# A retention layer and a Mish MLP on one core: the second tile's k turned back ahead of its outputs, with markers and one transpose moved

## The chip, the core and the metric

The kernel runs on one core of a Trainium2 chip. The metric is the device time of one execution in microseconds (us); lower is better. Engines: PE (TensorE, matmuls; PEld is its weight load), DVE (VectorE), ACT (ScalarE), POOL (GpSimd) and SP (SyncE). POOL and SP issue most of the DMAs. Each engine takes its instructions in the order in which the program gives them, and waits on semaphores for the others.

## The reference

```python
scores = (q @ k.T) / sqrt(64)                 # 8 batches, 8 heads, 576 positions, head size 64
rel = pos[:, None] - pos[None, :]
ret = scores * where(rel >= 0, gamma[h] ** rel, 0)      # gamma[h] = 1 - 2 ** (-5 - h)
x = (ret @ v).transpose(0, 2, 1, 3).reshape(4608, 512)
h = x @ w_in                                  # 512 -> 2048
g = h * tanh(softplus(h))                     # Mish
out = g @ w_out                               # 2048 -> 512, float32
```

## The kernel before

**Work and tiles.** The 4608 rows are 36 chunks of 128, four to a tile, nine tiles (t = 0 to 8). Chunks 0 to 7 are the first 128 positions of each batch; they make tiles 0 and 1 and are computed directly (scores, mask, outputs). The later chunks use a running state per batch: scores inside halves of 64 positions, plus the state times q. Each tile then goes through `g1` (x times w_in by 16 blocks of 128 columns, Mish on ACT) and a second product with w_out: tile 0 by `g2_first`, the others by `unit`, seven products of halves (Strassen) whose sums DVE makes (`g_sum`, L645 to 653, and `w_sum`).

**First chunks.** For tile t, `f_transpose` makes q and k by head, `f_scores` the masked scores, `f_v` (L221) casts v of one chunk from float32 to bf16 (L226), and `f_out` (L229; products at L242) makes the outputs, on L251 copied to the tile's xT. `f_k0` (L259, 16 transposes on PE at L264) turns k back into rows, `f_k0_copy` (L267) copies that from PSUM into two tiles, `first_states` (L277, L289) multiplies it with v, and `first_states_copy` (L297) puts the result into SBUF as the first state. `f_out` for tile 1 and `f_k0` both draw from the two buffers named `sc`. Their letters in the list of steps (L853): T `f_transpose`, S `f_scores`, C `f_mix`, V `f_v`, O `f_out`, F `f_state`. Step i of that list stands ahead of part i of tile 0's `g2_first` (four row blocks s of four parts); `store` copies a finished row block out (L619) and sends it.

**Loads.** `load(n)` (L308) issues chunk n's q, k and v from POOL (L325). From chunk 10 on, a tiny POOL copy stands ahead of it (L313) that waits until the v of chunk n - 2 has landed. The loads of chunks 8 to 11 are given at L843, before tile 0's `g1` and `g2_first`.

**Later chunks.** For chunk n: P (`step_p`, DVE, L341) scales q and k, V (`step_v`, L348) scales v, T (`step_t`, L351) transposes, below chunk 16 on PE (L362) and from 16 on by a DMA that SP issues (L370). A visit (`visit`, or `visit_first` and `visit_second`) makes two chunks' outputs: products L484, then L500 for one set of row halves, a marker, other products, and L500 for the other set; the output copies are L512 on ACT. The marker (`written`, L411) is an empty instruction on SP's queue that waits for the last products of the first set; the first product of the second set waits for the marker (`behind`, L406). `first_states` uses a marker in the same way.

**Order.** It is written out by hand: the loops at L854 (g2 of tile 0), L886 (steps u of tile 1's g1, then tile 1's first units) and L951 (tiles 2 on) give every engine its queue. SP's queue has the transposing DMAs (L370), the sends of output rows (L611) and the markers; POOL's has the loads, the L313 copies, later the V steps and the pacing copies (L949).

Of the kernel before, what the change touches and what calls it, by code (L numbers as in the profile page):

```python
# [10 lines left out]
BF16 = mybir.dt.bfloat16  # L11
# [5 lines left out]
def kernel(  # L17
# [18 lines left out]
    nc = tc.nc  # L36
    B, H, S, D = q.shape
    assert (B, H, S, D) == (8, 8, 576, 64)
    P = 128
    NP = H // 2  # L40
# [5 lines left out]
    NPE = 16  # L46
# [17 lines left out]
    first = ctx.enter_context(tc.tile_pool(name="first", bufs=1))  # L64
    io = ctx.enter_context(tc.tile_pool(name="io", bufs=PF))
    tok = ctx.enter_context(tc.tile_pool(name="tok", bufs=6))
    tr = ctx.enter_context(tc.tile_pool(name="tr", bufs=4))
# [99 lines left out]
    k0 = {}  # L167
# [3 lines left out]
    def f_mix(g, i):  # L171

        name = ("qb", "kb")[i]
        fst[1][name, "mix", g] = room[3][:, ts(i, 1024)].rearrange("p (r x d) -> p r x d", r=8, x=2)
        nc.vector.tensor_copy(fst[1][name, "mix", g].rearrange("p r x d -> p x r d"),
                              fst[1][name][:, ds(2 * g, 2), :].rearrange("p x (r d) -> p x r d", r=8))
# [44 lines left out]
    def f_v(t, b, copy):  # L221
        vb = room[2][:, ts(b, 512)].rearrange("p (h d) -> p h d", h=H)
        copies = copy if isinstance(copy, tuple) else (copy,)
        n = H // len(copies)
        for j, copy in enumerate(copies):
            copy(vb[:, ds(n * j, n), :], v0[4 * t + b][:, ds(n * j, n), :])  # L226
        fst[t]["vb"][b] = vb
# [25 lines left out]
    def f_state(t, b, engine=nc.gpsimd):  # L253

        n = 4 * t + b
        v0s[n] = room[(6, 3)[t]][:, ts(b, H * D)].rearrange("p (h d) -> p h d", h=H)
        engine.tensor_tensor(v0s[n], v0[n], gv[:, 0, :].unsqueeze(2).to_broadcast([P, H, D]), op=OP.mult)

    def f_k0(t):  # L259

        tp = ps_sc.tile([P, 2, H, P], BF16, name="sc")
        for g in range(2):
            for h in range(H):
                nc.tensor.transpose(tp[:, g, h, :], fst[t]["kb", g][:, h, :], ident)  # L264
        return tp

    def f_k0_copy(t, tp, copies):  # L267
        for g in range(2):
            pair = first.tile([P, 2, H, D], BF16, name="k0", bufs=2)
            copies[g](pair.rearrange("p x h d -> p h x d"), tp[:, g].rearrange("p h (x d) -> p h x d", x=2))  # L270
            for x in range(2):
                k0[4 * t + 2 * g + x] = pair[:, x]

    s0 = {}
    s0_banks = {}

    def first_states(t, j):  # L277

        if j == 0:
            s0_banks[t] = [pool.tile([P, 2, NP, 64], F32, name=name)  # L280
                           for pool, name in ((ps_st, "st"), (ps_o, "ops"))]
        made = []
        for x in range(2):
            for p in range(NP):
                for i in range(2):
                    r, b = ds(64 * (i ^ j), 64), 4 * t + 2 * i + x
                    for e in range(2):
                        hh = 4 * (p // 2) + 2 * e + p % 2
                        made.append(nc.tensor.matmul(  # L289
                            s0_banks[t][i][ds(64 * e, 64), x, p, :], lhsT=k0[b][r, hh, :], rhs=v0s[b][r, hh, :],  # L290
                            start=(j == 0 and x == 0 and p == 0), stop=True, skip_group_check=True))
        if j == 0:
            s0_banks[t].append(written(made[-8:]))
        else:
            behind(made[0], s0_banks[t][2])

    def first_states_copy(t, copy):  # L297
        for i in range(2):
            pair = first.tile([P, 2, NP, 64], F32, name="s0", bufs=4)
            copy(pair, s0_banks[t][i])  # L300
            for x in range(2):
                s0[4 * t + 2 * i + x] = pair[:, x]
# [103 lines left out]
    def behind(ins, others):  # L406

        sync = mybir.DependencyInfo(mybir.DependencyClass.Sync, mybir.DependencyReason.DATA)
        tc.add_manual_dep(ins.ins, others.ins.name, sync, reason="row halves and a bank")

    def written(products):  # L411
        sync = mybir.DependencyInfo(mybir.DependencyClass.Sync, mybir.DependencyReason.DATA)
        seen = nc.sync.nop()
        for ins in products:
            tc.add_manual_dep(seen.ins, ins.ins.name, sync, reason="row halves and a bank")
        return seen
# [53 lines left out]
    def run(jobs, *how):  # L470
        while jobs:
            jobs.pop()(*how)
# [152 lines left out]
    NS = 2  # L625
# [39 lines left out]
    dve, act, pool = nc.vector.tensor_copy, nc.scalar.copy, nc.gpsimd.tensor_copy  # L665
# [122 lines left out]
    def att(n, steps):  # L788
        if n >= n_chunks:
            return  # L790
        for step in steps:
            {"P": step_p, "V": step_v, "T": step_t}[step](n)
# [46 lines left out]
    for j in range(2):  # L839
        half = mask[ds(64 * j, 64)]  # L840
# [9 lines left out]
        g1(0, f)  # L850
    for i in range(2):
        f_mix(0, i)
    steps = {0: "T0", 3: "S0 C1", 9: "T1", 11: "S1", 12: "V0 V1 V2 V3", 14: "O0 O1 O2 O3", 15: "F0 F1"}  # L853
    for i in range(nF):  # L854
        for step in steps.get(i, "").split():
            n = int(step[1])
            if step[0] == "T":
                for j in range(2):
                    f_transpose(1, n, j, [(ps_sc, "sc", (dve, act)[j])])
            elif step[0] == "S":  # L860
                f_scores(1, n)
            elif step[0] == "V":
                f_v(1, n, dve if n == 3 else act)
            elif step[0] == "C":
                for j in range(2):
                    f_mix(n, j)
            elif step[0] == "F":
                f_state(1, n, nc.vector)
            else:
                f_out(1, n, (dve, act)[n // 2])  # L870
        g2_first(i // 4, i % 4)
# [10 lines left out]
    ps = {0: 0, 4: 1, 8: 2, 11: 3}  # L882
    vs = {0: 0, 5: 1, 9: 2, 13: 3, 18: 4, 19: 5}
    ts_ = {4: 0, 7: 1, 12: 2, 14: 3, 19: 4, 21: 5}
    FIRST = {1: (0, 0), 2: (1, 0), 3: ("turn", 1), 5: (0, 1), 6: (1, 1)}
    for u in range(24):  # L886
        j, w = divmod(u, 4)
        halved[0] = 2 if u < 1 else 0
        if u in FIRST:
            what, of = FIRST[u]  # L890
            if what == "turn":
                f_k0_copy(of, f_k0(of), (dve, act))
            else:
                first_states(of, what)
                if what:
                    first_states_copy(of, act)
        if u in ps:
            att(N0 + ps[u], "P")
        if u == 11:
            step_m(N0)  # L900
        if u in vs:
            att(N0 + vs[u], "V")
        if u in (1, 2):
            f_state(1, u + 1, nc.vector)
        for what in {7: "W4", 9: "W6 W3 W1", 19: "S1", 21: "S6"}.get(u, "").split():
            w_sum(int(what[1])) if what[0] == "W" else g_sum(1, int(what[1]))
        if w == 0 and j > 0:
            if j < 5:
                load(N0 + j + 3)
            else:  # L910
                more_loads(N0 + j + PF)
        if u == 10:
            units = states(N0)
            units[0]()
            step_s(N0)
            units[1]()
            run(sums)
        elif u == 16:
            att(N0 + 4, "P")
            visit(N0, ((ps_o, "ops"), (ps_h, "hp")), (act, act), masked=False)  # L920
            g_sum(1, 2)
            run(sums)
            att(N0 + 5, "P")
            step_m(N0 + 2)
        elif u == 22:
            visit(N0 + 2, ((ps_h, "hp"), (ps_h, "hp")), (act, act))
        if u in (13, 20):
            run(casts, dve if u == 13 else act)
        if u in ts_:
            att(N0 + ts_[u], "T")  # L930
        if u < nF:
            g1(1, u)
            flush()
        else:
            unit(1, u - nF)


    PLAN, ALONE = ([x.split() for x in y.split("|")] for y in (
        "S2 g0 g1 U0|S1 U1|g2 g3 U2|U3|g4 g5 U4|U5|g6 U6|S6 g7|U7 g8 g9|S5 U8|U9 g10|g11|S7 g12 g13 U10|U11|g14 U12|g15 U13",
        "S2 g0 g1 U0|S1 U1|g2 g3 U2|U3|g4 g5 U4|U5|g6|S6 g7 U6|U7 g8 g9|S5 U8|U9 g10|g11|S7 g12 g13 U10|U11|g14 U12|U13 g15"))  # L940
# [10 lines left out]
    for t in range(NS, nT):  # L951
        for i in range(nF):
            n, w = NCH * (t + 1) + i // 8 * 2, i % 8
# [2 lines left out]
                run(casts, act)  # L956
            if (t, i) in HALVED:
                halved[0] = HALVED[t, i]
            for job in PLAN[i] if t > NS else {5: ("S5",), 8: ("W7",), 9: ("S7",)}.get(i, ()):
                if job[0] == "S":  # L960
                    g_sum(t - 1, int(job[1]))
                elif job[0] == "W":
                    w_sum(int(job[1]))
# [30 lines left out]
            if n + 2 >= NPE and w == (6 if n + 2 == NPE else 3) and n + 4 < n_chunks:  # L994
                tick(t, i)
                att(n + 4, "V")
                att(n + 5, "V")
            if w == 7 and n + 4 == NPE:
                att(n + 5, "T")
            if w == (4 if n <= NPE - 2 else 7) and n + 4 >= NPE:  # L1000
                att(n + 4, "T")
# [65 lines left out]
```

## Time and profile before

| | |
|---|---|
| median of three runs | 290.27 us (290.06 to 297.87) |
| the profiled execution | 289.96 us, span 288.2 us |
| PE busy | 280.8 us, 97% of the span |
| DVE, ACT, POOL busy | 200.1, 156.8, 156.3 us |
| mean granted PE clock | 1.000 |
| PE waits listed | 1.3 us at the start; 0.7, 0.6 and three of 0.2 later |

The span runs from the first to the last instruction; the time of an execution is a little longer. Times in the views count from the span's start. A timeline row has start, duration, engine, source line, operation, output and inputs, and a count of merged instructions; in brackets, the idle time before it and what ended it.

### The profile page before, as it was taken

How to read it: one execution, taken by the hardware profiler on the slowest of the kernel's cores; microseconds unless marked ns; L12 is line 12 of the kernel's file. 1: busy time of each engine (PE TensorE's matmuls, PEld its weight loads, DVE VectorE, ACT ScalarE, POOL GpSimd, SP SyncE). 2: the span in 40 equal slices, each digit the busy share in tenths (PEclk: the TensorE clock that was granted, in tenths of full speed). 3: DMA queues.
4: the chain of work that ended last, by engine and by line, in shares of the span. 5: the costliest groups of instructions: out<-in, count | busy, mean ns of one | idle time of the engine just before them, and what ended most of it. 6: DMA issues, size and time to landing. Idle time of an engine off the chain costs nothing.

```text
span 288.2 us, 8782 instructions
## 1 busy us (share of the span) xinstructions
PE 280.8 (97%) x3812; PEld 188.7 (65%) x3812; DVE 200.1 (69%) x281; ACT 156.8 (54%) x272; POOL 156.3 (54%) x226
## 2 busy tenths in 40 slices
PE   8899999999999999999999999999999999999994
PEld 3466775556876657666766666667666766665783
DVE  4741457999999987895599767975895272533383
ACT  5566414788776564565465555564466446444320
POOL 8686860887793999697929685969140000000000
PEclk9999999999999999999999999999999999999999
DMA  7999999988899994999898994696937001201133
GB/s 150 198 204 205 205 238 220 292 200 197 191 210 196 166 283 121 161 217 196 210 168 184 178 238 136 182 198 182 176 90 131 2 3 73 75 1 73 28 102 93
DMA packets 41543, 45.93 MB, mean 159 GB/s; under 512 B 23840, under 2 KB 31264, under 8 KB 41504
## 3 DMA queue, kind: packets, MB, share of 16 engines
q0 software_dynamic: 14256, 30.15, 49.6%
q1 hardware_dynamic: 26656, 14.69, 26.3%
q8 instruction: 30, 0.49, 0.8%
q10 hardware_dynamic: 592, 0.52, 0.6%
q14 instruction: 9, 0.07, 0.1%
HBM read 36.70 MB, written 9.44 MB: 160 GB/s over the span
## 4 chain that ended last, share of the span: by engine, by line
PE 82%; DMA 12%; POOL 3%; issue 1%; DVE 1%; ACT 0%; POOLq 0%; ACTq 0%
PE hp L570 38%; PE ops L661 30%; DMA room<-in_v_dram 5%; DMA w_out_t<-in_moe_w_out_dram 4%; DMA gT<-in_v_dram 3%; PE hp L661 2%; PE sc L428 2%; POOL gT L107 2%; PE sc L382 2%; PE sc L752 1%; PE st L661 1%; PE hp L575 1%; PE hp L500 1%; PE sc L362 1%; PE hp L484 1%
## 5 line engine op out<-in xcount | busy, mean ns | idle before, releaser
L570 PE MATMUL hp<-xT,w_in_t 128*128 128x512 bf16 x530 | 128.7, 380 | 0.1
L586 ACT ACTIVATE gT<-hp 128x512 bf16<-128x512 f32 x144 | 85.9, 600 | 54.6 <-PE hp L570 53.1
L570 PEld LDWEIGHTS <-w_in_t 128*128 128x128 bf16 x530 | 50.8, 98 | 45.7 <-issue 0.5
L661 PEld LDWEIGHTS <-room 128*128 128x128 bf16 x608 | 58.8, 98 | 14.7
L341 DVE TENSOR_TENSOR qks<-qkraw,gqk 128x512 bf16<-128x512 f32 x56 | 48.1, 909 | 8.9 <-issue 7.4
L652 DVE TENSOR_TENSOR room<-gT 128x2048 bf16<-128x2048 bf16 x40 | 49.5, 1259 | 0.8 <-ACT gT L586 0.8
L661 PE MATMUL ops<-room,room 128*128 128x256 bf16 x336 | 41.7, 273 | 0.0
L949 POOL COPY held<-gT 128x1 bf16<-128x1 bf16 x58 | 24.4, 421 | 31.2 <-ACT gT L586 31.2
L661 PEld LDWEIGHTS <-gT 128*128 128x128 bf16 x256 | 24.5, 98 | 6.2 <-issue 0.2
L388 DVE TENSOR_TENSOR sm<-sc,mask 128x1024 bf16<-128x1024 f32 x14 | 17.1, 1218 | 14.9 <-PE sc L382 12.6
L661 PE MATMUL ops<-w_out_t,room 128*128 128x256 bf16 x224 | 27.1, 273 | 0.0
L348 POOL TENSOR_TENSOR vs<-vraw,gv 128x512 bf16<-128x512 f32 x20 | 26.0, 1320 | 0.0
L325 POOL DMA_DIRECT2D vraw<-in_v_dram x24 | 21.3, 887 | 3.6 <-DMA w_out_t<-in_moe_w_out_dram 2.6
L325 POOL DMA_DIRECT2D qkraw<-in_q_dram x24 | 21.7, 904 | 1.0 <-issue 0.6
L325 POOL DMA_DIRECT2D qkraw<-in_k_dram x24 | 21.2, 883 | 0.0
L452 DVE TENSOR_TENSOR total<-sc,total 128x256 f32<-128x256 f32 x32 | 13.5, 423 | 2.2 <-PE sc L428 1.4
L512 ACT CAST xT<-hp 128x512 bf16<-128x512 f32 x19 | 10.3, 589 | 7.3 <-PE hp L500 7.3
L575 PE MATMUL hp<-xT,w_in_t 128*128 128x256 bf16 x92 | 13.8, 273 | 0.0
L661 PE MATMUL ops<-room,gT 128*128 128x256 bf16 x112 | 13.4, 273 | 0.0
L575 PEld LDWEIGHTS <-w_in_t 128*128 128x128 bf16 x92 | 9.0, 98 | 5.5
L661 PE MATMUL ops<-w_out_t,gT 128*128 128x256 bf16 x96 | 12.3, 273 | 0.0
L696 DVE TENSOR_TENSOR res<-ops,res 128x512 f32<-128x512 f32 x6 | 4.2, 692 | 9.0 <-PE ops L661 9.0
(162 smaller groups left out, 339.8 us busy)
## 6 DMA issues: line engine op xcount, KB each, us to landing
out_dram<-res SPq DMA_DIRECT2D x29, 256.0 KB, 4.7
qkraw<-in_q_dram POOLq DMA_DIRECT2D x24, 256.0 KB, 5.9
qkraw<-in_k_dram POOLq DMA_DIRECT2D x24, 256.0 KB, 6.8
vraw<-in_v_dram POOLq DMA_DIRECT2D x24, 256.0 KB, 6.1
w_out_t<-in_moe_w_out_dram POOLq DMA_DIRECT2D x4, 512.0 KB, 10.2
w_in_t<-in_moe_w_in_dram POOLq DMA_DIRECT2D x3, 512.0 KB, 9.3
out_dram<-res SPq DMA_DIRECT2D x9, 128.0 KB, 2.3
gT<-in_k_dram POOLq DMA_DIRECT2D x8, 128.0 KB, 9.1
```

The costliest lines, as they stand in the source:

```text
L325: nc.gpsimd.dma_start(out=t, in_=src[b, :, ds(P * c, P), :].rearrange("h p d -> p h d"))
L341: nc.vector.tensor_tensor(slots[:, :, y], heads[:, :, y], factors[:, :, y].unsqueeze(3).to_broadcast([P, NP, 2, D]), op=OP.mult)
L348: engine.tensor_tensor(vs, live[n]["v"], gv[:, c, :].unsqueeze(2).to_broadcast([P, H, D]), op=OP.mult)
L388: nc.vector.tensor_tensor(sm.rearrange("p e x n i -> p (e x n) i"), live[n]["sc"].rearrange("p e x n i -> p (e x n) i"), mask.unsqueeze(1) ...
L452: nc.vector.tensor_tensor(new[:, k], st[:, j, x], total[b], op=OP.add)
L512: copy(xts[t][:, :, ds(P * s, 2 * P)].rearrange("p h (x j i) -> p j h x i", x=2, j=2)[:, j], both[j])
L570: nc.tensor.matmul(to, lhsT=w, rhs=x, start=first, stop=last)
L575: nc.tensor.matmul(to[:, ts(j, n)], lhsT=w, rhs=x[:, ts(j, n)], start=False, stop=False, skip_group_check=True)
L586: nc.scalar.activation(gts[t][:, f, :], hp, AX.Mish)
L652: engine.tensor_tensor(to, g_half(t, *a), g_half(t, *b), op=op_)
L661: nc.tensor.matmul(bank[:, half, :], lhsT=g[:, f, ts(half, P)], rhs=w[:, f, :], start=(f == 0 and half == 0 and not add), stop=(f == hF - ...
L949: nc.gpsimd.tensor_copy(held[:, i % 2:i % 2 + 1], gts[t][:, f, 0:1])
```

## The change

1. Tile 1's k is turned back (`f_k0` and `f_k0_copy`) at step 13 of tile 0's g2, between V1 and V2, and not at step u = 3 of tile 1's g1. Both copies are on DVE (before: one DVE, one ACT), into two buffers of the pool `qkT` (before: into the two `k0` buffers that tile 0 uses).
2. V2 and V3 move from step 12 to step 13; V3's cast is on POOL (before: DVE).
3. The markers of the visits stand on ACT's queue; those of `first_states` stay on SP's.
4. In tile 2's loop, chunk 17's T comes at step 5 (before: 7), and the sum S5 at step 6 (before: 5).

```diff
--- before.py
+++ after.py
@@ -266,7 +266,11 @@
 
     def f_k0_copy(t, tp, copies):
         for g in range(2):
-            pair = first.tile([P, 2, H, D], BF16, name="k0", bufs=2)
+            if t == 0:
+                pair = first.tile([P, 2, H, D], BF16, name="k0", bufs=2)
+            else:
+                pair = tr.tile([P, 2, NP, P], BF16, name="qkT", bufs=6)
+                pair = pair.rearrange("p i n t -> p (i n t)").rearrange("p (x h d) -> p x h d", x=2, h=H)
             copies[g](pair.rearrange("p x h d -> p h x d"), tp[:, g].rearrange("p h (x d) -> p h x d", x=2))
             for x in range(2):
                 k0[4 * t + 2 * g + x] = pair[:, x]
@@ -290,7 +294,7 @@
                             s0_banks[t][i][ds(64 * e, 64), x, p, :], lhsT=k0[b][r, hh, :], rhs=v0s[b][r, hh, :],
                             start=(j == 0 and x == 0 and p == 0), stop=True, skip_group_check=True))
         if j == 0:
-            s0_banks[t].append(written(made[-8:]))
+            s0_banks[t].append(written(made[-8:], nc.sync))
         else:
             behind(made[0], s0_banks[t][2])
 
@@ -408,9 +412,9 @@
         sync = mybir.DependencyInfo(mybir.DependencyClass.Sync, mybir.DependencyReason.DATA)
         tc.add_manual_dep(ins.ins, others.ins.name, sync, reason="row halves and a bank")
 
-    def written(products):
+    def written(products, engine=nc.scalar):
         sync = mybir.DependencyInfo(mybir.DependencyClass.Sync, mybir.DependencyReason.DATA)
-        seen = nc.sync.nop()
+        seen = engine.nop()
         for ins in products:
             tc.add_manual_dep(seen.ins, ins.ins.name, sync, reason="row halves and a bank")
         return seen
@@ -850,7 +854,7 @@
         g1(0, f)
     for i in range(2):
         f_mix(0, i)
-    steps = {0: "T0", 3: "S0 C1", 9: "T1", 11: "S1", 12: "V0 V1 V2 V3", 14: "O0 O1 O2 O3", 15: "F0 F1"}
+    steps = {0: "T0", 3: "S0 C1", 9: "T1", 11: "S1", 12: "V0 V1", 13: "K1 V2 V3", 14: "O0 O1 O2 O3", 15: "F0 F1"}
     for i in range(nF):
         for step in steps.get(i, "").split():
             n = int(step[1])
@@ -860,7 +864,9 @@
             elif step[0] == "S":
                 f_scores(1, n)
             elif step[0] == "V":
-                f_v(1, n, dve if n == 3 else act)
+                f_v(1, n, pool if n == 3 else act)
+            elif step[0] == "K":
+                f_k0_copy(n, f_k0(n), (dve, dve))
             elif step[0] == "C":
                 for j in range(2):
                     f_mix(n, j)
@@ -882,18 +888,15 @@
     ps = {0: 0, 4: 1, 8: 2, 11: 3}
     vs = {0: 0, 5: 1, 9: 2, 13: 3, 18: 4, 19: 5}
     ts_ = {4: 0, 7: 1, 12: 2, 14: 3, 19: 4, 21: 5}
-    FIRST = {1: (0, 0), 2: (1, 0), 3: ("turn", 1), 5: (0, 1), 6: (1, 1)}
+    FIRST = {1: (0, 0), 2: (1, 0), 5: (0, 1), 6: (1, 1)}
     for u in range(24):
         j, w = divmod(u, 4)
         halved[0] = 2 if u < 1 else 0
         if u in FIRST:
-            what, of = FIRST[u]
-            if what == "turn":
-                f_k0_copy(of, f_k0(of), (dve, act))
-            else:
-                first_states(of, what)
-                if what:
-                    first_states_copy(of, act)
+            half, of = FIRST[u]
+            first_states(of, half)
+            if half:
+                first_states_copy(of, act)
         if u in ps:
             att(N0 + ps[u], "P")
         if u == 11:
@@ -956,7 +959,7 @@
                 run(casts, act)
             if (t, i) in HALVED:
                 halved[0] = HALVED[t, i]
-            for job in PLAN[i] if t > NS else {5: ("S5",), 8: ("W7",), 9: ("S7",)}.get(i, ()):
+            for job in PLAN[i] if t > NS else {6: ("S5",), 8: ("W7",), 9: ("S7",)}.get(i, ()):
                 if job[0] == "S":
                     g_sum(t - 1, int(job[1]))
                 elif job[0] == "W":
@@ -995,7 +998,7 @@
                 tick(t, i)
                 att(n + 4, "V")
                 att(n + 5, "V")
-            if w == 7 and n + 4 == NPE:
+            if w == 5 and n + 4 == NPE:
                 att(n + 5, "T")
             if w == (4 if n <= NPE - 2 else 7) and n + 4 >= NPE:
                 att(n + 4, "T")
```

## What was predicted

> **What bounds the kernel now.** I read the page first (busy shares, the 40 slices), then who waits for whom with TensorE as the waiter, then the timelines of PE, POOL and DVE around the edited steps. The page first:
>
> ```profile
> span 288.2 us, 8782 instructions
> ...
> PE 280.8 (97%) x3812; PEld 188.7 (65%) x3812; DVE 200.1 (69%) x281; ACT 156.8 (54%) x272; POOL 156.3 (54%) x226
> ...
> PEclk9999999999999999999999999999999999999999
> ```
>
> PE is busy almost everywhere, at full granted clock. Whatever makes PE wait in mid-kernel is added to the end, since nothing later has room to give it back; and there is little idle time to win. In the stage that is edited there is one PE wait. The waits view lists it as 0.6 us on ACT L226, the cast of a first-chunk v (step V2), and the PE timeline shows where it lies:
>
> ```profile
> 44.61 1.89 PE L570 MATMUL hp<-w_out_t,gT 128*128 128x512 bf16 x8
> 46.43 0.64 PE L242 MATMUL sc<-room,room 128*64 128x128 bf16 x16
> 47.70 0.64 PE L242 MATMUL sc<-room,room 128*64 128x128 bf16 x16 [0.63 <-ACT room L226]
> 48.27 1.04 PE L570 MATMUL ops<-w_out_t,gT 128*128 128x512 bf16 x4
> ...
> 53.57 1.06 PE L264 MATMUL sc<-ident,qkT 128*128 128x128 bf16 x16
> ```
>
> L242 at 46.43 is O0 and O1, at 47.70 O2 and O3 (8 matmuls each, so O3 starts near 47.91), L264 at 53.57 is the turned-back k. Eight 128x512 products issue in 44.61 to 46.34, 0.216 us each. Now the engine to which the change hands one cast, POOL:
>
> ```profile
> 42.42 0.88 POOL L325 DMA_DIRECT2D vraw<-in_v_dram  x1 [2.62 <-DMA w_out_t<-in_moe_w_out_dram]
> 50.65 0.63 POOL L313 COPY landed<-vraw 128x1 f32<-128x1 f32 x1 [7.35 <-DMA vraw<-in_v_dram]
> 51.23 0.89 POOL L325 DMA_DIRECT2D qkraw<-in_q_dram  x1
> 52.11 0.88 POOL L325 DMA_DIRECT2D qkraw<-in_k_dram  x1
> 52.98 0.88 POOL L325 DMA_DIRECT2D vraw<-in_v_dram  x1
> 53.86 0.43 POOL L313 COPY landed<-vraw 128x1 f32<-128x1 f32 x1
> 54.23 0.88 POOL L325 DMA_DIRECT2D qkraw<-in_q_dram  x1
> 55.10 0.88 POOL L325 DMA_DIRECT2D qkraw<-in_k_dram  x1
> 55.98 0.88 POOL L325 DMA_DIRECT2D vraw<-in_v_dram  x1
> ```
>
> POOL looks idle from 43.3 to 50.65, but it is not free: it stands at the L313 copy of load(10), waiting for chunk 8's v to land, and everything later in its queue stands behind it. The loads of chunks 8 to 11 (L843) are issued in the program before the g2 loop at L854, so the moved cast V3 comes behind all nine of these rows: the instruction order of the changed kernel has it after the vraw issue of chunk 11. The casts and DVE:
>
> ```profile
> L226 POOL CAST room<-gT x2: 520/566/612, 13.3 to 15.3; 128x512 bf16<-128x512 f32 x1, 128x256 bf16<-128x256 f32 x1
> ...
> L226 DVE CAST room<-room x1: 427/427/427, 47.1 to 47.1; 128x512 bf16<-128x512 f32 x1
> ```
> ```profile
> 43.84 2.35 DVE L219 TENSOR_TENSOR room<-sc,dmask 128x1024 bf16<-128x1024 f32 x2 [1.44 <-PE sc L212]
> 47.07 0.43 DVE L226 CAST room<-room 128x512 bf16<-128x512 f32 x1 [0.88 <-DMA room<-in_v_dram]
> ```
>
> Before, V3 (the DVE row at 47.07) is done at 47.50, ahead of O3.
>
> **The change part by part.**
>
> *V3 on POOL.* The source landed at 46.95, so only POOL's queue counts. POOL is past the last of the nine rows at 55.98 + 0.88 = 56.86. The 128x512 cast takes 0.61 there (the longer of the two L226 POOL casts), so V3 is done at 57.47, and O3 starts 0.05 later (ACT's cast ended at 47.65 and O2 began at 47.70): 57.52 against 47.91. **Delay of PE at O3: 9.6 us.** Behind O3 on PE stand the last two row blocks of g2, all of the next g1 and everything else; DVE and ACT then wait for PE. The chain does not depend on PE: its DMAs and nine POOL rows need nothing made after 46 us. Its bounds: chunk 8's v could land earlier or later (third rival); the second landing, chunk 9's v, has its last piece at 52.84 in the trace's record of landings, 1.0 us before POOL asks for it. Behind V3 on POOL stands the L313 copy for chunk 10, which before ran at 59.07 after 2.2 us of waiting, so it loses nothing.
>
> *The clock after the gap.* PE would stand from about 48.2 (O2's end, below) to 57.5, 9.3 us. The trace's clock record has two entries, 1.0 from 6.34 us on and 0.5 from 289.65, 5.4 us after the last matmul ended. A 9.3 us gap is longer, so I take it that the clock falls and PE restarts at half pace. The price is in the first row of PE:
>
> ```profile
> 1.26 5.26 PE L164 MATMUL ops<-room 128*128 128x512 bf16 x12 [1.26 <-DVE room L126]
> ```
>
> These 12 products took from 1.26 to about 6.35, 5.1 us; at 0.216 each they would have taken 2.6. **Cost 2.5 us**, bounds 0 (the clock stays) and 2.5. I take 2.5, the only cold stretch in the trace. [...]
>
> *The 16 turn-backs (L264), moved from 53.57 to before the second row block of g2's last quarter.* Their 0.89 us (53.57 to 54.46) leaves the path after O3. In the new place, 45.47 to 46.36, they only shorten the wait for V3: **gain 0.9 us**. They need the score buffer that the first L219 frees near 45.0; free. If V3 were on time they would cost what they gain.
>
> *Their two copies.* Both now on DVE, ahead of L251 (before: one on DVE, 0.68, one on ACT, 1.01, off the path). O2 and O3 take the same score buffer as the turn-backs, so O2 now waits for the copies: DVE ends L219 at 46.19, copies out a row block (L619, 0.68), then two of 0.68, done near 48.0. O1 ends near 47.74, so O2 waits some 0.3 us. Cover: the wait for V3; 0 on the path, 0.3 if that cover is gone. V2's old wait is gone too (ready 47.65), which the 9.6 already holds.
>
> *The copies' new buffers.* Two more of the six qkT buffers are drawn; what they held was last read by the first tile's scores, before 20 us. Later transposes draw buffers whose readers are done. Cost 0, the range of it nothing.
>
> *Markers on ACT.* Fourteen markers of the visits go from SP's queue to ACT's; the two of the first states stay. On SP they made PE wait once, some 0.08 us at 98.93. On ACT a marker stands behind whatever ACT has not finished: before the second half at 77.71 ACT's last copy ends at 77.69, at 156.13 at 156.15; elsewhere it is 0.1 us or more ahead. What is queued behind the marker on ACT, the visit's own output copies (L512), needs later matmuls anyway. Bounds -0.1 to +0.6 (one ACT copy in the way once); I take +0.1. SP's transposes and sends, freed of these waits, wait for DVE as before.
>
> *Chunk 17 sooner, S5 after it.* The transposing DMA on SP now follows P17 at step 5 instead of 7; its readers come near 99 and it landed before that already: 0. But S5 (L652) now stands behind P17 on DVE:
>
> ```profile
> 86.53 1.22 DVE L652 TENSOR_TENSOR room<-gT 128x2048 bf16<-128x2048 bf16 x1
> 87.67 1.29 DVE L341 TENSOR_TENSOR qks<-qkraw,gqk 128x512 bf16<-128x512 f32 x2
> ```
>
> Swapped, S5 ends near 86.5 + 1.2 + 1.2 = 88.9, and the products that read it began at 88.79: +0.1 (0 to 0.8, the latter if P17's rows landed late).
>
> **Sum.** 9.6 + 2.5 - 0.9 + 0.1 + 0.1 = +11.4 us on the profiled execution's 289.96 us (span 288.2): **301.4 us**. Its time is 0.3 us under the median of the three runs, 290.27; against that it is 3.8% more.
>
> **Rivals.**
> *The clock does not fall.* Same wait, warm restart: 301.4 - 2.5 = 298.9. For it: no mid-kernel gap in this trace shows a fall. Against: the end of the trace does, after 5.4 us. 0.08.
> *A second landing waits too.* If the DMA of chunk 9's v takes what the slowest vraw took (13.5 us from issue to landing, median 6.1), it lands at 56.8, not 52.84; POOL goes on 2.9 us later, and so does O3: 304.3. Against: its landing is on record and nothing ahead of it changes but one earlier store. 0.10.
> *The other side: chunk 8's v lands before POOL asks.* If it were there by 43.3, the rows from 50.65 to 56.86 (6.2 us) and the cast would end at 50.1, O3 would be 2.3 us late, the gap too short for the clock: 289.96 + 2.3 - 0.9 + 0.2 = 291.6, no change. It decides at a landing near 46.7, 4 us earlier than now, where the gap gets under 5.4 us and the total under 2%. Against: the same loads queue ahead of it as before. 0.05.
> *The change does what it looks like.* POOL takes V3 at 46.95 as if its queue were empty: O2 starts near 48.1 for the copies, g2 goes on 0.4 us later than before, and 0.9 is saved: 289.7. Only if the order on POOL were another. 0.01.
>
> **How the numbers follow.** The forecast has 0.76. The range, 298.5 to 304.3, takes in the warm restart below and the late second landing above, and the small terms. 2% (5.8 us) is about what a measurement of this kernel can tell from no change. Slower by over 2%: 0.76 + 0.08 + 0.10 = 0.94. Within 2%: 0.05. Faster: 0.01.
>
> **What would show it.** Right: in the changed profile a PE wait of some 9 us at L242 on POOL L226, that cast on POOL near 57 behind nine unchanged rows, a digit under 9 in PEclk near 58, 128x512 products at 0.43 us for some 5 us, and the rest of PE's timeline shifted by about 11 us without new gaps. The turn-backs stand near 45.5 with both copies on DVE. Wrong: V3 on POOL before 52, or later PE gaps above 0.5 us at L500 (markers) or at the products of S5 near 100.

## The result, and the profile after

The changed kernel takes 300.67 us (median of six runs) against 290.16 us before (six runs): 1.034 times as long, 95% interval 1.030 to 1.038. 301.4 was predicted, with a range from 298.5 to 304.3. The profiled execution took 300.16 us (span 298.5) against 289.96 (288.2). Some executions of most kernels here, the kernel before among them, were disturbed and ran up to 20 us longer; all ratios below leave those out, and so may differ from a ratio of medians.

The changed kernel's page and its list of PE's waits (us in total, times, longest):

```profile
PEclk9999999599999999999999999999999999999998
```
```profile
PE sc L242 <- POOL room L226: 8.2, 1, 8.2
```

PE has one long wait, 8.2 us for POOL's cast; the next in the list are 1.3 us at the start and 0.5. The granted clock is low in the slice from 52 to 60 us (each slice is 7.5 us). Lines of the changed kernel below the edit are four higher than before (L325 is L329, L313 is L317, L570 is L574). PE's timeline comes first, then POOL's. The last view has two stretches, each with its length, the busy times of PE, PEld, DVE, ACT and POOL, then the granted clock (0.50 and 1.00), the DMA share and GB/s:

```profile
45.07 1.06 PE L264 MATMUL sc<-ident,qkT 128*128 128x128 bf16 x16
...
46.92 0.64 PE L242 MATMUL sc<-room,room 128*64 128x128 bf16 x16
47.73 0.41 PE L242 MATMUL sc<-room,room 128*64 128x128 bf16 x8 [0.17 <-ACT res L623]
56.38 0.64 PE L242 MATMUL sc<-room,room 128*64 128x128 bf16 x8 [8.24 <-POOL room L226]
```
```profile
49.86 0.19 POOL L317 COPY landed<-vraw 128x1 f32<-128x1 f32 x1 [8.33 <-DMA vraw<-in_v_dram]
...
52.95 0.20 POOL L317 COPY landed<-vraw 128x1 f32<-128x1 f32 x1
...
55.70 0.63 POOL L226 CAST room<-room 128x512 bf16<-128x512 f32 x1
```
```profile
56.38:61.00 4.62, 4.29 (x18) 1.91 (x20) 2.13 (x4) 1.43 (x2) 3.10 (x5) 0.50 0.97 208
61.00:66.00 5.00, 4.95 (x91) 2.74 (x91) 5.00 (x9) 3.53 (x8) 3.73 (x4) 1.00 0.88 271
```

The order is the one foreseen: turn-backs, O0 and O1, O2, then eight microseconds of nothing, because V3 on POOL has its turn only after two landing waits and six issues. Behind the wait PE runs at half clock for 4.6 us. The trace's clock record has it low from 50.78, 2.6 us after O2's end, to 61.02.

Where the time went is best seen from three marks on PE: O3's first product, the first product of L500 in the first visit, and the last product of all. The columns are the time of O3, then the two stretches, in us (differences of start times in the profiled executions; "gap filled" and the others are the experiments below):

| kernel | O3 | O3 to first visit | first visit to last product |
|---|---|---|---|
| before | 47.95 | 21.72 | 214.34 |
| changed | 56.38 | 23.07 | 214.81 |
| changed, second profile | 56.56 | 23.43 | 214.69 |
| only V3 on POOL | 56.21 | 24.16 | 214.94 |
| two loads behind V3 | 48.10 | 20.86 | 214.85 |
| one load behind V3 | 53.78 | 23.49 | 217.48 |
| gap filled, second profile | 56.83 | 20.85 | 217.38 |
| turn-backs, V3 on ACT | 47.89 | 20.95 | 215.15 |

Changed less before: 8.43 + 1.35 + 0.47 = 10.25 us, the whole difference of the spans (10.2). (The second profile is of the same kernel in another run, below.) In the second column stand two terms: without the turn-backs at their old place and at full clock it is 20.9 (three kernels), so they give back 0.8 to 0.9 and the half clock costs 2.2 to 2.6. That fits the clock record: 4.6 us of work at a clock of 0.50 would lose 2.3.

### The profile page after: what moved, and what is told of

It reads as the page before. It is cut to its first block, busy times and chain, and to the rows that moved or that the text cites. A ratio compares the mean times of both kernels' runs of the same rounds, so it can differ in the third digit from the quotient of the medians.

```text
span 298.5 us, 8749 instructions
## 1 busy us (share of the span) xinstructions
PE 280.6 (94%) x3774; PEld 189.2 (63%) x3812; DVE 202.8 (68%) x281; ACT 156.6 (52%) x271; POOL 160.0 (54%) x227
## 4 chain that ended last, share of the span: by engine, by line
PE 79%; DMA 11%; POOL 6%; issue 1%; DVE 1%; POOLq 0%
PE hp L574 36%; PE ops L665 29%; DMA vraw<-in_v_dram 4%; DMA w_out_t<-in_moe_w_out_dram 4%; DMA gT<-in_v_dram 3%; PE hp L665 2%; POOL qkraw L329 2%; PE sc L432 2%; POOL gT L107 2%; PE sc L386 1%; PE st L665 1%; PE sc L756 1%; PE hp L579 1%; PE hp L504 1%; PE sc L366 1%
## 5 line engine op out<-in xcount | busy, mean ns | idle before, releaser
L574 PE MATMUL hp<-xT,w_in_t 128*128 128x512 bf16 x498 | 126.1, 380 | 1.6
L590 ACT ACTIVATE gT<-hp 128x512 bf16<-128x512 f32 x144 | 85.8, 599 | 55.9 <-PE hp L574 51.0
L574 PEld LDWEIGHTS <-w_in_t 128*128 128x128 bf16 x530 | 50.9, 98 | 46.2 <-issue 0.8
L345 DVE TENSOR_TENSOR qks<-qkraw,gqk 128x512 bf16<-128x512 f32 x56 | 49.6, 936 | 6.9 <-issue 4.8
L656 DVE TENSOR_TENSOR room<-gT 128x2048 bf16<-128x2048 bf16 x40 | 49.4, 1258 | 0.9 <-ACT gT L590 0.8
L952 POOL COPY held<-gT 128x1 bf16<-128x1 bf16 x58 | 28.7, 518 | 33.4 <-ACT gT L590 33.4
L329 POOL DMA_DIRECT2D qkraw<-in_q_dram x24 | 24.5, 1020 | 8.3 <-DVE qks L345 7.5
L329 POOL DMA_DIRECT2D vraw<-in_v_dram x24 | 22.0, 933 | 2.2 <-DMA w_out_t<-in_moe_w_out_dram 1.3
L329 POOL DMA_DIRECT2D qkraw<-in_k_dram x24 | 23.1, 963 | 0.0
L456 DVE TENSOR_TENSOR total<-sc,total 128x256 f32<-128x256 f32 x32 | 13.5, 422 | 2.2 <-PE sc L432 1.4
L317 POOL COPY landed<-vraw 128x1 f32<-128x1 f32 x8 | 6.6, 821 | 10.9 <-DMA vraw<-in_v_dram 10.9
```

What stands on the lines that cost most here:

```text
L329: nc.gpsimd.dma_start(out=t, in_=src[b, :, ds(P * c, P), :].rearrange("h p d -> p h d"))
L345: nc.vector.tensor_tensor(slots[:, :, y], heads[:, :, y], factors[:, :, y].unsqueeze(3).to_broadcast([P, NP, 2, D]), op=OP.mult)
L456: nc.vector.tensor_tensor(new[:, k], st[:, j, x], total[b], op=OP.add)
L574: nc.tensor.matmul(to, lhsT=w, rhs=x, start=first, stop=last)
L590: nc.scalar.activation(gts[t][:, f, :], hp, AX.Mish)
L656: engine.tensor_tensor(to, g_half(t, *a), g_half(t, *b), op=op_)
```

## Experiments

Theory: V3 queues on POOL behind two landing waits, and the gap lets the clock fall. Rivals: the moved turn-backs, with their copies on DVE and the shared score buffer, hold the outputs; the markers on ACT hold PE at each visit; a cast on POOL is slow by itself.

**V3 back on DVE.**

```diff
-                f_v(1, n, pool if n == 3 else act)
+                f_v(1, n, dve if n == 3 else act)
```

> The changed kernel with V3's cast back on DVE, all else as changed. Queue theory (V3 waits on POOL behind two landing waits and six loads, and the gap lets the clock fall): the wait of 8.2 us at O3 goes and the clock stays up. DVE now makes V3 behind the two turn-back copies, near 48.4, so O3 starts about 0.5 us later than before the change and the turn-backs' 0.9 us are saved later: 289.8 us, ratio to before 0.996 to 1.002. Rival (the turn-backs ahead of the outputs, their score buffer and their copies are what holds O2 and O3): about 300 us, nearly unchanged. Rival (markers on ACT cost something at each of 14 visits): above 291.

Measured: 1.002 (0.999 to 1.006). One word undoes the whole loss, so neither the turn-backs nor the markers hold the outputs. But there is a new PE wait of 1.6 us, from 88.6 us on. DVE and PE in this kernel:

```profile
87.65 1.29 DVE L345 TENSOR_TENSOR qks<-qkraw,gqk 128x512 bf16<-128x512 f32 x2 [1.57 <-DMA qkraw<-in_k_dram]
88.86 1.22 DVE L656 TENSOR_TENSOR room<-gT 128x2048 bf16<-128x2048 bf16 x1
```
```profile
90.14 1.05 PE L665 MATMUL ops<-w_out_t,room 128*128 128x256 bf16 x8 [1.57 <-DVE room L656]
```

P17 (L345) waits for chunk 17's k, S5 (L656) stands behind it, and the products of S5 wait for S5. In the changed kernel the same P17 began without a wait and S5 was done at 98.51, ahead of its products at 99.02: the load of this k was issued only 1.7 us later there than before the change (82.29 against 80.56), while PE was some 10 us behind, so the loads had gained a lead on PE.

**Only V3 on POOL**, in the kernel before.

```diff
-                f_v(1, n, dve if n == 3 else act)
+                f_v(1, n, pool if n == 3 else act)
```

> The kernel before with one word changed: V3's cast on POOL, still at step 12. Queue theory: V3 ends near 56.3 as in the changed kernel, O3 starts 8.5 us later than before, the clock falls (2.3 us in the changed kernel's profile), and the turn-backs stay where they were, so their 0.9 us is not saved: 289.96 + 8.5 + 2.3 = 300.8 us, ratio 1.03 to 1.04, that is as slow as the changed kernel or 1 us slower. Rival (turn-backs and copies): 290, ratio 1.00.

Measured: 1.038 (1.032 to 1.043). Its PE:

```profile
56.21 0.64 PE L242 MATMUL sc<-room,room 128*64 128x128 bf16 x8 [9.06 <-POOL room L226]
```

The one word alone makes the whole loss. The wait is longer by what the turn-backs no longer fill (9.1 against 8.2), and they cost their 0.9 at the old place as well.

**Two loads behind V3**, V3 still on POOL.

```diff
-    for b in range(4):
+    for b in range(2):
         load(N0 + b)
...
                 f_v(1, n, pool if n == 3 else act)
+                if n == 3:
+                    for b in (2, 3):
+                        load(N0 + b)
```

> The changed kernel with V3 still on POOL, but the loads of chunks 10 and 11 given behind V3 and not ahead of it. Queue theory: POOL is free when the source lands near 46.9, V3 ends near 47.6, O2 waits for the turn-back copies until 48.1, the clock stays up: 289.5 us, ratio 0.995 to 1.002. The loads lose 0.6 us at most, as they wait until 49.9 for a landing anyway. Rival (a cast on POOL is slow or late by itself, whatever stands ahead of it): near 300 us. Rival (turn-backs and copies): near 300 us.

Measured: 1.004 (0.998 to 1.010), the profiled execution among the shortest (span 287.9). POOL, then PE:

```profile
45.87 0.61 POOL L226 CAST room<-room 128x512 bf16<-128x512 f32 x1 [3.77 <-DMA room<-in_v_dram]
```
```profile
47.88 0.64 PE L242 MATMUL sc<-room,room 128*64 128x128 bf16 x16 [0.17 <-ACT res L623]
```

The same cast on the same engine, 0.6 us long, ends before O2 starts. It is the queue ahead of it, not the engine.

**One load behind V3**, a step between the changed kernel and the one just shown.

```diff
-    for b in range(4):
+    for b in range(3):
         load(N0 + b)
...
                 f_v(1, n, pool if n == 3 else act)
+                if n == 3:
+                    load(N0 + 3)
```

> The changed kernel with one of the two loads that stand ahead of V3 on POOL (chunk 11's: an L313 copy and three DMA issues) given behind it. Queue theory, by dose: V3 comes 2.9 us sooner (0.2 + 3 x 0.88 and a little), near 52.8, O3 near 53.5, the wait 5.3 us and not 8.2. The clock still falls, as it did 2.6 us after PE stopped in the changed kernel: 296.6 to 297.8 us, ratio 1.021 to 1.026. Rival (only the first landing wait or POOL itself matters, not the number of issues): near 300 or near 290.

Measured: 1.039 (1.031 to 1.047), no better than the changed kernel, and so a miss in time. In the trace the wait is the one expected:

```profile
53.78 0.64 PE L242 MATMUL sc<-room,room 128*64 128x128 bf16 x8 [5.33 <-POOL room L226]
...
217.79 0.26 PE L504 MATMUL sc<-qkT,ssb 64*64 64x64 bf16 x8 [1.74 <-issue]
```

The wait is 5.3 us, O3 comes 2.8 us sooner than in the second profile of the changed kernel, and at the first visit the lead is still 2.7. It is lost behind that, 1.7 us of it where PE stands at 216 us for nothing that the profile shows ("issue"), 0.4 at such a stop at 208, the rest in smaller steps. Only one execution was profiled; whether the others lost it in the same way stays open.

**PE kept at work in the gap.** The result of the added products is not used.

```diff
+                if n == 3:
+                    keep_warm(34, ps_h, "hp")
                 f_out(1, n, (dve, act)[n // 2])
```

> The changed kernel with 34 products 128x512 whose result is not used (7.3 us at 0.216 us each) on PE between O2 and O3, so that PE works while it waits for V3. Queue theory with the clock as a term of its own: the wait stays, O3 starts at the same time near 56.4, but at full clock, and the 2.3 us of half pace behind it go: 298.2 us, ratio to before 1.025 to 1.031, granted clock 1.0 throughout. Rival (the clock's fall costs nothing, since PE would have waited for something else then): 300 us or more. If the added work delayed PE by itself: above 301 us.

Measured: 1.035 (1.028 to 1.042), against 298.2 us (1.025 to 1.031) expected, so the total does not show the gain. In the profiled execution (304.0 us) the clock stays at 1.0 across the gap and PE takes 20.85 us from O3 to the first visit, but further on it stops for 1.2 and 2.0 us without a shown cause. The changed kernel and this one were then run side by side:

> The changed kernel as it is, once more, for comparison on the same chip with the next three. 300 to 301.5 us, ratio 1.034: V3 on POOL near 55.7, a wait of 8.2 us at O3, the clock down from about 50.8 to 61.

Measured: 1.038 (1.033 to 1.044), the clock down from 51.70 to 61.94.

> The changed kernel with 34 products 128x512, not used, on PE between O2 and O3, a second time, since the first profile of it started 1 us late and held two stops of PE that have nothing to do with the change. If the clock's fall is a cost of its own (2.3 us at half pace): 298.3 us, that is 0.991 to 0.994 of the changed kernel, and granted clock 1.0 throughout. If it costs nothing: equal to the changed kernel.

Measured: 1.030 (1.022 to 1.038); medians 300.02 and 301.37. The intervals overlap, so the times alone do not settle it. PE:

```profile
48.32 7.51 PE L164 MATMUL hp<-room 128*128 128x512 bf16 x34
56.83 0.41 PE L242 MATMUL sc<-room,room 128*64 128x128 bf16 x8 [1.00 <-POOL room L226]
```

O3 comes 0.3 us later, the clock stays at 1.0, and from O3 to the first visit PE takes 20.85 us and not 23.43: the clock's fall costs 2.6 us there. From the first visit on this execution loses 2.7 us against the changed kernel, nearly all at two stops without a shown cause (1.4 and 0.7), which hides the gain in its total. They are at the same two matmuls as the stops of the first profile, so they may come with the added products.

**The other parts alone.** Markers (in the kernel before: `written` on ACT's queue for the visits):

> The kernel before with the visits' markers on ACT's queue and nothing else. My sum: +0.1 us (-0.1 to +0.6), ratio 0.999 to 1.002, and no PE gap above 0.3 us at the second set of a visit's products (L500). Rival (each of 14 markers stands behind ACT work and holds PE): 14 gaps, 2 us or more, ratio above 1.006.

Measured: 1.006 (1.002 to 1.010). Against that stands the profiled execution: 290.04 us and no wait at any marker. Counted from the first visit, every visit up to 200 us comes within 0.2 us of the kernel before, the one at 207 within 0.3; the other 0.6 of the 1.0 us that this stretch takes longer is one stop without a shown cause at 206.55. A cost of the markers of more than 0.3 us is not to be seen there; what makes the interval's 0.6% is open.

Chunk 17's transpose and S5 (in the kernel before: the lines of change 4):

> The kernel before with chunk 17's transposing DMA at step 5 and S5 at step 6 of tile 2, and nothing else. The trace of the changed kernel shows S5 on time, but there POOL's loads had eight more microseconds of lead. Without the wait at V3, theory: S5 stands on DVE behind P17, and P17 behind the landing of chunk 17's k, so PE waits at the products of S5: 0.1 us when the k has landed, up to 1.6 us (as in the run with V3 on DVE) when it has not. Ratio 1.000 to 1.006. Rival (the wait of 1.6 us there came from the turn-backs or the markers): no PE wait at the products of S5, ratio 1.000.

Measured: 1.014 (1.010 to 1.018), more than either theory gave, and by another wait. PE:

```profile
90.75 0.42 PE L500 MATMUL hp<-qkT,ssb 64*64 64x64 bf16 x16 [2.44 <-SPq L413]
```

S5 was on time here. With the markers still on SP, the sooner transpose stands ahead of visit 12's marker on that queue: it is issued at 87.52 and holds SP for 3.1 us, and the marker comes at 90.69, where before it stood ahead of the transpose and came at 88.48. PE waits 2.4 us for it, and the clock falls for one stretch of 3.4 us. In the runs that have both moves no marker holds PE, so it is the markers' move that makes chunk 17's move possible.

**Towards a version without the loss.** V3 on ACT behind V2, all else as changed:

> The changed kernel with V3's cast on ACT behind V2. Queue theory: V3 ends near 47.5, O2 waits for the turn-back copies until 48.1, nothing waits for V3, the clock stays up: 289.5 us if chunk 17's k lands in time, up to 1.6 us more if not; ratio 0.996 to 1.004. Rival (the turn-backs ahead of the outputs cost by themselves): above 1.01.

Measured: 1.003 (0.998 to 1.007). In the profiled execution (298.1 us) the products of S5 wait 1.5 us again. The place behind P17 is only half of that cause; the other is when chunk 17's k lands. It landed at 86.63 here and at 87.56 with V3 on DVE, but at 85.60 in the run with two loads behind V3. There V3 was in time and S5 stood behind P17 just the same, and S5's products waited 0.2 us. DVE in that run, then its line in the list of PE's waits:

```profile
85.87 1.28 DVE L345 TENSOR_TENSOR qks<-qkraw,gqk 128x512 bf16<-128x512 f32 x2
87.08 1.21 DVE L656 TENSOR_TENSOR room<-gT 128x2048 bf16<-128x2048 bf16 x1
```
```profile
PE ops L665 <- DVE room L656: 0.2, 1, 0.2
```

V3 on ACT, with S5 back at step 5 as well:

> The changed kernel with V3 on ACT, and S5 back at step 5 of tile 2, ahead of P17 on DVE; chunk 17's transpose stays sooner, the markers on ACT. If the 1.5 us wait at the products of S5 seen with V3 on ACT or DVE comes from S5 standing behind P17: no PE wait there, 289.2 to 290 us, ratio 0.996 to 1.001, the same as the turn-backs alone. If the markers cost something at each visit: above 290.5.

Measured: 1.001 (0.996 to 1.005). PE does not wait for S5 here (its one wait of 0.2 us for a sum, L656, is for another one, at 77.4 us). But k had landed at 84.80, so S5 would have been in time behind P17 too, and this run does not show that the place alone was at fault. And the turn-backs with V3 on ACT, without the other parts:

> The kernel before with the turn-backs moved as in the change and V3 on ACT; the markers stay on SP, and chunk 17 and S5 stay where they were. Theory: the 0.6 us wait for V2 and the 0.9 us of the turn-backs at their old place are traded for 0.9 us at the new place, 0.2 to 0.4 us of wait for their copies: 0.4 to 0.6 us faster than before, ratio 0.997 to 1.000. Rival (turn-backs in the new place hold the outputs): slower by more than 1 us.

Measured: 1.000 (0.997 to 1.003), no gain. The 0.8 us is there at the first visit (20.95 against 21.72) and is given back by 107 us. ACT in the kernel before, then in this one:

```profile
106.74 0.58 ACT L681 COPY res<-ops 128x512 f32<-128x512 f32 x1 [1.86 <-DMA out_dram<-res]
```
```profile
106.91 0.59 ACT L685 COPY res<-ops 128x512 f32<-128x512 f32 x1 [2.54 <-DMA out_dram<-res]
```

Both copies wait for the same send of output rows, which ends near 106.8 in both. PE came sooner and then waited 0.3 us for the PSUM bank that this copy empties, and 0.2 before that, at 77.4, for one of DVE's sums. No version tried is faster than the kernel before.

## Why the prediction was right, step by step

- **V3 on POOL.** Right, and the whole loss. Predicted delay at O3 9.6 us, measured 8.4. The size was 1.2 too large, since the chain of nine rows is no constant: chunk 8's v landed 0.8 us sooner (49.86 against 50.65), and the two L313 copies took 0.19 and 0.20 us, not 0.63 and 0.43.
- **The clock.** Predicted 2.5, measured 2.2 to 2.6. The step was right, its reason a little off: the fall came 2.6 us after PE's last work, and not after 5.4 us as at the end of the trace of before. The size fitted partly by luck: the 5.1 us at half rate at the kernel's start are no measure of a restart, and behind the gaps of these runs work went on at half clock for 2.8 to 5.5 us.
- **Turn-backs.** Predicted 0.9 saved behind O3; 0.8 to 0.9 measured. That O2 would wait some 0.3 us, covered by the wait for V3, held too (0.17). The view puts that wait down to ACT's copy L623, done at 47.61, of which O2 reads nothing; the second turn-back copy, whose score buffer O2 takes, was done at 47.58. So that it was the copies is the likelier reading, not a shown one.
- **Markers.** Predicted +0.1; in the changed kernel no visit's second set waits. Alone, 0 to 0.3 in the trace. The 0.08 us at 98.93 that the prediction puts down to a marker on SP lies within the first set of that visit, ahead of its marker (99.31).
- **S5 behind P17.** Predicted +0.1 (0 to 0.8); 0 in the changed kernel. Where V3 is in time it was 0.2 with two loads behind V3, but 1.5 and 1.6 with V3 on ACT and on DVE, by when k landed. The upper bound was too small: it let k land 0.7 us late at most. And it was priced as if it stood by itself, while in the changed kernel the wait at V3 covered it.
- **Chunk 17 sooner.** Predicted 0: right beside the markers' move, and wrong without it (2.4 us and the clock). The prediction did not name that dependence.
- **What was not foreseen:** 0.4 us at 92.43, PE's stop without a shown cause, in place of the two terms of 0.1. The second profile has no such stop and is still 0.35 behind, in small steps.

Of the rivals, the other side needed a landing near 46.7; it came at 49.7. The second landing (chunk 9's v) came at 52.22, ahead of POOL's copy at 52.95, which did not wait. That rival's price was also too high: counted from its issue at 42.42, as the view counts, 13.5 us end at 55.9 and not at 56.8, so 303.5 us and not 304.3. That the clock stays up was wrong in every kernel with the gap left open (waits of 5.3 to 9.1 us).

## What to carry to other kernels

An engine that shows no work may be standing at a wait, as POOL did here for 8.3 us up to 49.86: before you hand it something urgent, read what its next instructions wait for, and count the issues between. Where a cast goes onto a queue with landing waits, give the loads behind it (two of them here: 1.004 times the time before, not 1.034). Price the parts of a change together: here the wait at V3 could hide a wait of up to 1.6 us at S5, and chunk 17's move was safe only beside the markers' move (2.4 us of wait without it).

## What the runs showed of the hardware

**The clock's steps.** The low stretches in mid-kernel were 10.24 us in the changed kernel, 6.83 with one load behind V3 and 3.41 with chunk 17 alone, where PE had waited only 2.4 us: 3, 2 and 1 times 3.413. The stretches at full clock between them in the changed kernel, 44.37 and 235.52, are 13 and 69 times as much. A low stretch began 2.0 to 4.2 us after the start of the last matmul before the stop, and ended 2.8 to 5.5 us after work resumed (2.9 and 4.6 in the changed kernel). The shortest stops with a fall behind them were 2.0 us (first profile with the gap filled) and 2.4 (chunk 17 alone); the longest without one were 1.7 (one load behind V3) and 1.6 (V3 on DVE). What sets the step no run shows.

**PE's stops without a shown cause.** Past the first 20 us, and counted from one matmul's start to the next, those of over 0.45 us are up to 4.4 us long. They lie near the same places in the instruction stream, whatever product stands there: at matmul 1117 in both profiles with a filled gap (and near it in the changed kernel), at 2908 in two, at 3036 or 3037 in six of the profiles, and once at 2525. (For one of the two at 2908 the view names a small POOL copy, L952.) From 1117, 2525 and 2908 to 3036 there are 1919, 511 and 128 matmuls, which is 15, 4 and 1 times 128 within one matmul. Counted in steps of 128 matmuls from the start, 1117, 2908, 3036 and 2525 are 8.73, 22.72, 23.72 and 19.73. The longest, in the profile with V3 on ACT:

```profile
212.74 0.32 PE L504 MATMUL sc<-qkT,ssb 64*64 64x64 bf16 x8 [4.21 <-issue]
```

The queue that the page lists as "q8 instruction" moves 30 packets of 16 KB, and PE's 3812 matmuls are 29.8 such steps. Each of these stops ended 1.2 to 1.7 us after such a packet had landed (in the changed kernel at 92.94, after a landing at 91.73), and the number landed by then was the whole part of the figure above: 8, 22, 23 and 19. In the kernel before, which does not stop at 3036, the 23rd packet had landed 4.5 us ahead. The place near 3036 lies in visits, where 64x64 products issue fast (16 of them from 207.89 to 208.03 in the profile with V3 on ACT, 9 ns each). What PE waited for at these stops no run shows.
